# Attention and a gated feed-forward on one core: heads of a pair interleaved, transfers merged, and the planner's due times shifted

## The chip, the core and the metric

The kernel runs on one core of a Trainium2 chip. The metric is the device time of the whole program in microseconds. Before the change three runs took 1405.53, 1406.59 and 1406.96 us; the median is 1406.59 us.

## The reference

Attention over 8 batches, 12 heads, 448 positions and 64 channels, with q and k normalized by their root mean square, is followed by a two-layer network on 3584 tokens of 768 channels. The network's weights are drawn in double precision, q, k and v in single precision.

```python
q_n, k_n = rmsnorm(q, g_q), rmsnorm(k, g_k)
scores = q_n @ k_n.T / sqrt(64)
attn = exp(scores - max(scores))          # per row
attn = attn / (sum(attn) + 1e-9)
x = (attn @ v), heads put side by side    # 3584 x 768
h = x @ w_in                              # 3584 x 2048
out = (h * cos(h)) @ w_out                # 3584 x 768
```

## The kernel before

Heads are taken in 48 pairs, u = 0 to 47; a batch b is six pairs. Everything is held with channels on the partitions: one pair's q or k is a tile of 128 partitions (head 0's 64 channels, then head 1's) by 448 or 512 positions.

The first six pairs are "plain": their products are done in full single precision. All later pairs split each operand into a high part in the reduced format fp32r and the rest, a low part, and add two or three fast products. For a later pair, `prepare(u)` loads statistics input `sd`, k (`kd`) and q (`qd`), computes the norms (ACT squares, DVE reduces, GpSimd, named POOL, takes the power), sends the k norms to DRAM and back to spread them over partitions (`rkb`), scales k and q, and splits them: `khi`, `kl`, `qhi`, `ql`. Transfers then place them head by head: M holds a head's high k over its low k (64 partitions each), D the high q twice, E the low q. One matmul of M with D and one with E then give the complete score. M, D and E are rings of three heads.

`attend(u)` goes on: `score` (line 496 on) writes one of three PSUM banks S; `rowmin` (DVE, line 514) scales a tile of scores and takes its extreme; `expo` (ACT, line 522) writes the probabilities P and their sum. `transp` (lines 557 to 565) turns P in four chunks kc, each in two banks PT0 (four tiles) and PT1 (three). ACT casts a turned chunk to `hi` (`pt_high`, line 579), DVE subtracts to `lo` (`pt_low`, lines 586 and 588), and `av` (line 603) multiplies both with the split v into banks O0 and O1, one for each head. The ring of `hi` has two chunks, that of `lo` one. At the end of a pair `x_half` (ACT, line 637) copies half of an O bank into `xf` and `x_sum` (DVE, line 642) adds its other half; `x_norm` (POOL) applies the row sums. The next pair's first product needs the same two O banks.

`multiply(b)` computes h of a batch in 16 blocks fc of 18 matmuls each (`ffn1`, lines 672 to 674) in one PSUM bank `ph`; `h_out` (ACT, line 689) copies a block to one of two buffers `he`, and `h_store` writes it to DRAM, 224 KB each. `weights` decodes the double-precision w_in, 16 stages; `weights2` decodes quadrants of w_out, adds and splits them and stores seven combinations for the second plan.

No engine has its program written out. `add` gives each part of the work (a part is one function call) an engine, a cost, a due time, the keys it reads and writes, and for a transfer its KB. `Plan.order` then runs a list schedule: when an engine is free it takes, of the parts whose inputs are ready by the planner's own clock, the one with the earliest due time. The result is the fixed order on every engine; at run time each engine works its list in order and waits on semaphores. Transfers are all issued from SP. There are two plans, one up to the last attention pair (to about 930 us), and one for the rest of x times w_in and the second layer, which replaces eight products of half-size blocks by seven.

Of the kernel before, what the change touches and what calls it, by code (L numbers as in the profile page):

```python
# [23 lines left out]
class Plan:  # L24
# [11 lines left out]
    SLACK = 0.0  # L36
# [33 lines left out]
    def order(self):  # L70
# [27 lines left out]
        moved = 0.0  # L98
        self.busy = dict.fromkeys(free, 0.0)
        while True:  # L100
# [42 lines left out]
def tile_attention_moe(  # L143
# [4 lines left out]
    qT: bass.AP,  # L148
    kT: bass.AP,
# [8 lines left out]
    B, S, D = 8, kT.shape[2], 64  # L158
# [26 lines left out]
    h_d = dpool.tile([B, NFC, 128, S], F32, tag="h_d", name="h_d")  # L185
# [7 lines left out]
    gs = cpool.tile([128, 3], F32, tag="gs", name="gs")  # L193
    gsc = gs[:, 2:3]
# [5 lines left out]
    def g_load():  # L200
        nc.sync.dma_start(gs[:, 0:2], gg)

    def g_fold():
        nc.vector.scalar_tensor_tensor(
            gs[:, 2:3], gs[:, 0:1], -float(D) / math.sqrt(D), gs[:, 1:2], op0=ALU.mult, op1=ALU.mult
        )
# [4 lines left out]
        "sd": 1, "r": 5, "rkb": 1, "kd": 1, "kl": 1, "khi": 1, "qd": 1, "ql": 1, "qhi": 1, "M": 3, "D": 3, "E": 3, "vd": 1, "vs": 2, "S": 3, "sm": 3, "P": 11,  # L211
        "hi": 2, "lo": 1, "O0": 1, "O1": 1, "xf": 6, "rs": 1, "rt": 1, "ph": 1, "xsb": 1, "he": 2, "wf": 2, "rn": 1,
        "aq": 4, "at": 2, "ao": 1,
# [3 lines left out]
    RING.update(dict.fromkeys(PKEYS, 1))  # L217

    def w_load(fc):
        if f64:  # L220
            st = raw[fc] = wpool.tile([128, 2 * DM], I32, tag=f"w{fc}", name=f"raw{fc}")
            nc.sync.dma_start(st, w_in[fc].bitcast(I32))
        else:
            wfl[fc] = apool.tile([128, DM], F32, tag="wf", name=f"wf{fc}", bufs=RING["wf"])
            nc.sync.dma_start(wfl[fc], w_in[fc])
# [17 lines left out]
    def w_decode(fc, step):  # L243
        if step == 0:
            wfl[fc] = apool.tile([128, DM], F32, tag="wf", name=f"wf{fc}", bufs=RING["wf"])
        decode(raw[fc], wfl[fc], step)
# [12 lines left out]
    stage, quad, temp, part = {}, {}, {}, {}  # L259
# [12 lines left out]
    def v_quad(c, k):  # L272
        quad[(c, k)] = apool.tile([128, HM], F32, tag="aq", name=f"aq{c}_{k}", bufs=RING["aq"])
# [6 lines left out]
    def v_sum(c, j):  # L280
        if j < 2:
            temp[(c, j)] = apool.tile([128, HM], F32, tag="at", name=f"at{c}_{j}", bufs=RING["at"])
        a21, a22, a11, a12 = (quad.get((c, k)) for k in range(4))
        if j == 0:
            nc.vector.tensor_tensor(temp[(c, 0)], a21, a22, ALU.add)
        elif j == 1:
            nc.vector.tensor_tensor(temp[(c, 1)], temp[(c, 0)], a11, ALU.subtract)
        elif j == 2:
            nc.vector.tensor_tensor(a21, a11, a21, ALU.subtract)
        else:  # L290
            nc.vector.tensor_tensor(a11, a12, temp[(c, 1)], ALU.subtract)

    def v_split(c, p, src, lo):
        f = temp[(c, src - 4)] if src > 3 else quad[(c, src)]
# [14 lines left out]
    qlow = [apool.tile([128, 384], F32R, tag=f"E{i}", name=f"E{i}", bufs=1) for i in range(RING["E"])]  # L309
# [17 lines left out]
    def e_clear(i):  # L327
        nc.vector.tensor_scalar(
            qlow[i][64:128], ident[64:128, 0:1].broadcast_to([64, 384]), 0.0, 0.0, op0=ALU.mult, op1=ALU.add
# [49 lines left out]
    def kn_norm(u):  # L379
        x = pair[u]["kn"][:KB].rearrange("p (t d) -> p t d", d=D)  # L380
# [18 lines left out]

    def rk_load(u):  # L400
        spread(tl(u, "rkb", [128, S], F32), rk_d[u].rearrange("p t -> (p t)"))

    def k_load(u):
        nc.sync.dma_start(tl(u, "kd", [128, S], F32), kT[u])

    def k_norm(u):
        kd = pair[u]["kd"]
        kn = tl(u, "km", [128, S], F32, "M") if u < NP else kd
        nc.gpsimd.tensor_tensor(kn, kd, pair[u].pop("rkb"), ALU.mult)

    def k_high(u):
        khi, kd = tl(u, "khi", [128, 512], F32R), pair[u]["kd"]
        nc.scalar.copy(khi[:, 64:], kd)
        nc.scalar.copy(khi[64:, :64], kd[64:, 384:])

    def k_low(u):
        d = pair[u]
        kl, kd, khi = tl(u, "kl", [128, 512], F32R), d.pop("kd"), d["khi"].bitcast(F32)
        nc.gpsimd.tensor_tensor(kl[:, 64:], kd, khi[:, 64:], ALU.subtract)
        nc.gpsimd.tensor_tensor(kl[64:, :64], kd[64:, 384:], khi[64:, :64], ALU.subtract)  # L420
# [4 lines left out]
    def q_load(u):  # L425
        q = q_plain(u) if u < NP else tl(u, "qd", [128, 512], F32)
        nc.sync.dma_start(q, qT[u])

    def q_scale(u):
        q = q_plain(u) if u < NP else pair[u]["qd"]  # L430
        nc.gpsimd.tensor_scalar(q, q, gsc, 0.0, op0=ALU.mult, op1=ALU.add)

    def q_high(u):
        nc.scalar.copy(tl(u, "qhi", [128, 512], F32R), pair[u]["qd"])

    def q_low(u):
        d = pair[u]
        nc.gpsimd.tensor_tensor(tl(u, "ql", [128, 512], F32R), d.pop("qd"), d["qhi"].bitcast(F32), ALU.subtract)

    def m_place(u, h, low):  # L440
        if not low:
            pair[u]["M", h] = apool.tile([128, S], F32R, tag="M", name=f"M{u}_{h}", bufs=RING["M"])
        src = pair[u]["kl" if low else "khi"].bitcast(F32)[64 * h : 64 * h + 64, 64 - 64 * h : 512 - 64 * h]
        nc.sync.dma_start(pair[u]["M", h].bitcast(F32)[64 * low : 64 * low + 64], src)

    def d_place(u, h):
        t = pair[u]["D", h] = apool.tile([128, 384], F32R, tag="D", name=f"D{u}_{h}", bufs=RING["D"])
        src = pair[u]["qhi"].bitcast(F32)[64 * h : 64 * h + 64, :384]
        for a in (0, 64):
            nc.sync.dma_start(t.bitcast(F32)[a : a + 64], src)  # L450

    def e_place(u, h):
        t = pair[u]["E", h] = qlow[(2 * u + h) % RING["E"]]
        nc.sync.dma_start(t.bitcast(F32)[:64], pair[u]["ql"].bitcast(F32)[64 * h : 64 * h + 64, :384])

    def v_load(u, hh):
        nc.sync.dma_start(tl(u, f"vd{hh}", [128, NVC, D], F32, "vd"), v[u, :, hh * NVC : hh * NVC + NVC])
# [740 lines left out]
```

## Time and profile before

| | us |
|---|---|
| median of three runs | 1406.59 |
| the profiled execution | 1406.09 |
| its span, first to last instruction | 1404.3 |
| PE busy in the span | 1361.3 (97%) |
| DVE busy | 1085.0 (77%) |
| ACT busy | 937.2 (67%) |
| POOL busy | 671.0 (48%) |

An engine's busy time is drawn from its instructions; PE's matmuls are pipelined and their ends are modelled. A releaser is what ended an engine's idle time. Names of tiles are the program's, so O is a second product of attention, PT a turned chunk, ph a block of h.

### The profile page before, as it was taken

How to read it: one execution, taken by the hardware profiler on the slowest of the kernel's cores; microseconds unless marked ns; L12 is line 12 of the kernel's file. 1: busy time of each engine (PE TensorE's matmuls, PEld its weight loads, DVE VectorE, ACT ScalarE, POOL GpSimd, SP SyncE). 2: the span in 40 equal slices, each digit the busy share in tenths (PEclk: the TensorE clock that was granted, in tenths of full speed). 3: DMA queues.
4: the chain of work that ended last, by engine and by line, in shares of the span. 5: the costliest groups of instructions: out<-in, count | busy, mean ns of one | idle time of the engine just before them, and what ended most of it. 6: DMA issues, size and time to landing. Idle time of an engine off the chain costs nothing.

```text
span 1404.3 us, 22489 instructions
## 1 busy us (share of the span) xinstructions
PE 1361.3 (97%) x6992; PEld 1184.7 (84%) x6992; DVE 1085.0 (77%) x1864; ACT 937.2 (67%) x1910; POOL 671.0 (48%) x676
## 2 busy tenths in 40 slices
PE   6998999999999999999989999999999999999998
PEld 2445788888888898888979799999999999999998
DVE  7898989687787978778796976517879979879843
ACT  6677787777877877887777787637547457467331
POOL 5779886867866777786687676220000000000000
PEclk9999999999999999999999999999999999999999
DMA  5678767687877788777868776319788468468334
GB/s 201 210 230 241 193 174 221 195 251 222 239 218 236 209 242 229 231 231 217 247 195 253 210 215 196 85 52 352 274 295 291 166 219 296 156 228 288 132 110 149
DMA packets 169479, 301.89 MB, mean 215 GB/s; under 512 B 28512, under 2 KB 123568, under 8 KB 169360
## 3 DMA queue, kind: packets, MB, share of 16 engines
q1 hardware_dynamic: 169360, 300.45, 69.4%
q8 instruction: 56, 0.92, 0.3%
q14 instruction: 63, 0.52, 0.1%
HBM read 193.59 MB, written 62.73 MB: 183 GB/s over the span
## 4 chain that ended last, share of the span: by engine, by line
PE 69%; DVE 17%; ACT 5%; issue 4%; POOL 3%; DMA 2%; SPq 0%; DVEq 0%; ACTq 0%; POOLq 0%
PE y L743 10%; PE y L742 10%; PE y L744 10%; PE O L603 6%; PE ph L672 6%; PE ph L673 6%; PE ph L674 6%; PE S L510 5%; PE PT L557 5%; DVE S L514 4%; DVE lo L586 2%; ACT P L522 1%; DVE hi L588 1%; DVE aq L237 1%; DVE aq L235 1%
## 5 line engine op out<-in xcount | busy, mean ns | idle before, releaser
L522 ACT ACTIVATE P<-S,sm 128x448 f32<-128x448 f32 x336 | 212.7, 635 | 98.1 <-DVE S L514 92.9
L672 PE MATMUL ph<-xs,wi 128*128 128x448 f32 x660 | 252.3, 382 | 1.1 <-ACT he L689 1.1
L742 PE MATMUL y<-g,wo 128*128 128x448 f32 x672 | 245.4, 365 | 0.0
L744 PE MATMUL y<-g,wo 128*128 128x448 f32 x672 | 245.4, 365 | 0.0
L743 PE MATMUL y<-g,wo 128*128 128x448 f32 x672 | 245.4, 365 | 0.0
L514 DVE TENSOR_SCALAR_CACHE_REDUCE S<-S,r 128x448 f32<-128x448 f32 x336 | 223.7, 684 | 25.0 <-PE S L510 18.7
L673 PE MATMUL ph<-xs,wi 128*128 128x448 f32 x660 | 242.0, 367 | 0.0
L674 PE MATMUL ph<-xs,wi 128*128 128x448 f32 x660 | 241.6, 366 | 0.0
L724 ACT CAST g<-gq 128x896 fp32r<-128x896 f32 x112 | 105.6, 943 | 177.5 <-PE y L744 174.8
L586 DVE TENSOR_TENSOR lo<-PT,hi 128x512 fp32r<-128x512 f32 x252 | 149.0, 614 | 82.1 <-ACT hi L579 69.2
L579 ACT CAST hi<-PT 128x512 fp32r<-128x512 f32 (+1 forms) x336 | 170.2, 534 | 52.3 <-PE PT L563 27.8
L722 DVE TENSOR_TENSOR g<-gq,g 128x896 fp32r<-128x896 f32 x112 | 121.9, 1089 | 69.0 <-ACT g L724 68.4
L557 PEld LDWEIGHTS PT<-ident,P 128*128 128x128 f32 (+1 forms) x1050 | 125.8, 140 | 37.2 <-issue 22.9
L557 PE MATMUL PT<-ident,P 128*128 128x128 f32 (+1 forms) x1050 | 152.0, 276 | 0.0
L672 PEld LDWEIGHTS ph<-xs,wi 128*128 128x128 f32 x660 | 124.3, 188 | 13.2 <-ACT he L689 3.9
L743 PEld LDWEIGHTS y<-g,wo 128*128 128x128 f32 x672 | 126.2, 188 | 10.0
L744 PEld LDWEIGHTS y<-g,wo 128*128 128x128 f32 x672 | 126.2, 188 | 10.0
L742 PEld LDWEIGHTS y<-g,wo 128*128 128x128 f32 x672 | 126.2, 188 | 10.0
L674 PEld LDWEIGHTS ph<-xs,wi 128*128 128x128 f32 x660 | 124.3, 188 | 10.6
L673 PEld LDWEIGHTS ph<-xs,wi 128*128 128x128 f32 x660 | 124.6, 189 | 8.6
L359 POOL TENSOR_TENSOR r<-r,nhalf 128x14 f32<-128x14 f32 (+1 forms) x48 | 124.2, 2587 | 4.0
L603 PE MATMUL O<-hi,vs 128*128 128x448 f32 x336 | 120.3, 374 | 3.4 <-DVE hi L588 2.9
(116 smaller groups left out, 2705.6 us busy)
## 6 DMA issues: line engine op xcount, KB each, us to landing
wo<-wo_d SPq DMA_DIRECT2D x152, 384.0 KB
gq<-h_d SPq DMA_DIRECT2D x64, 448.0 KB
h_d<-he SPq DMA_DIRECT2D x120, 224.0 KB
wo_d<-ao SPq DMA_DIRECT2D x56, 384.0 KB
sd<-sd SPq DMA_DIRECT2D x46, 448.0 KB
D<-qhi SPq DMA_DIRECT2D x168, 96.0 KB
raw<-w_in SPq DMA_DIRECT2D x16, 768.0 KB
rawo<-w_out SPq DMA_DIRECT2D x32, 384.0 KB
```

What stands on the lines that cost most here:

```text
L514: nc.vector.tensor_scalar(d["S", t][:, :S], d["S", t][:, :S], d["r"][:, t : t + 1], None, op0=ALU.mult, op1=ALU.min, accum_out=d["sm"][:, ...
L522: nc.scalar.activation(p_rows(u, t), d.pop(("S", t))[:, :S], AF.Exp, bias=sm[:, 1, t : t + 1], scale=-1.0, accum_out=sm[:, 2, t : t + 1],)
L557: nc.tensor.transpose(pt[part][:n, i * 128 : i * 128 + 128], p_rows(u, t)[:, c : c + n], ident)
L579: nc.scalar.copy(hi if kc < 3 else hi[:64], pt_rows(u, kc, part))
L586: nc.vector.tensor_tensor(lo, src, hi.bitcast(F32), ALU.subtract)
L603: nc.tensor.matmul(O, st, d[what, kc][:, HEADS[hh]], start=(kc + n == 0), stop=(kc == 3))
L672: nc.tensor.matmul(ph[:, :S], whi, x2[:, 0, :], start=(cc == 0), stop=False)
L673: nc.tensor.matmul(ph[:, :S], whi, x2[:, 1, :], start=False, stop=False)
L674: nc.tensor.matmul(ph[:, :S], wlo, x2[:, 0, :], start=False, stop=(cc == NCC - 1))
L742: nc.tensor.matmul(y, whi, hi[:, e], start=first and e == 0, stop=False, **more)
L743: nc.tensor.matmul(y, whi, lo[:, e], start=False, stop=False, **more)
L744: nc.tensor.matmul(y, wlo, hi[:, e], start=False, stop=last and e == NG - 1, **more)
```

## The change

**Layout.** From pair 6 on the host puts the two heads' channels in turn, so partition 2d + h holds channel d of head h, and k and q stand side by side in one input, `kq`. One transfer loads both. One transfer spreads the k norms. M, D and E now hold both heads of a pair side by side in 64 (or twice 64) partitions, two pairs deep, so one transfer, or two for M, places what four or two did. v is loaded and split whole.

**Buffers.** The spread norms use room in M (later pairs) or D (plain pairs), `kq` is one buffer, the quadrants of w_out use three work buffers instead of four and two, and w_out's fetches one instead of two. The ring of `lo` has two chunks instead of one. The two `he` buffers are one tile, and two blocks of h are stored in one transfer, after the second.

**Planner.** It now counts eight transfers in flight at most, has a few new costs, and adds to each due time a number from a table by kind of part and by stage (0: pairs 9 and later, 1: the first three later pairs, 2: plain pairs; for blocks of h, batch 0 apart). The second plan has no such table.

The diff, cut to its core:

```diff
     FLY = 5.0
-    SLACK = 0.0
+    LANES = 8
+    TWICE = ("rk_spread", "rs_load", "d_place", "m_place")
...
+        landed = [0.0] * self.LANES
...
             if kb:
-                moved = max(moved, end) + kb / self.RATE
                 fly = self.FLIGHT.get(fn.__name__, self.FLY) if t > 12.0 else 2.4
-                done = max(end + fly, moved + 1.2)
+                half = 1 + (fn.__name__ in self.TWICE)
+                for i in range(half):
+                    end = max(end if i else t, landed.pop(0)) + cost / half
+                    moved = max(moved, end) + kb / half / self.RATE
+                    done = max(end + fly, moved + 1.2)
+                    landed.append(done + self.SIGNAL[e])
+                free[e] = max(end, landed[0])
...
-        "hi": 2, "lo": 1, "O0": 1, "O1": 1, "xf": 6, "rs": 1, "rt": 1, "ph": 1, "xsb": 1, "he": 2, "wf": 2, "rn": 1,
-        "aq": 4, "at": 2, "ao": 1,
+        "hi": 2, "lo": 2, "O0": 1, "O1": 1, "xf": 6, "rs": 1, "rt": 1, "ph": 1, "xsb": 1, "he": 2, "wf": 1, "wg": 1, "rn": 1,
+        "a0": 1, "a1": 1, "a2": 1, "ao": 1,
...
+    qtwo, qlow, kboth = keep("D", 768), keep("E", 768), keep("M", 2 * S)
+    kq = apool.tile([128, S + 512], F32, tag="kq", name="kq", bufs=1)
+    kd, qd = kq[:, :S], kq[:, S:]
...
+    def rk_load(u):
+        row = rk_d[u].rearrange("p t -> (p t)").rearrange("(o h s) -> o h s", o=1, h=2)
+        nc.sync.dma_start(rkb(u), row.broadcast_to([64, 2, S]))
...
+    def kq_load(u):
+        nc.sync.dma_start(kq, kq_in[u])
...
     def k_high(u):
-        khi, kd = tl(u, "khi", [128, 512], F32R), pair[u]["kd"]
-        nc.scalar.copy(khi[:, 64:], kd)
-        nc.scalar.copy(khi[64:, :64], kd[64:, 384:])
+        nc.scalar.copy(tl(u, "khi", [128, S], F32R), kd)
...
+    def m_place(u, low):
+        src = pair[u]["kl" if low else "khi"].bitcast(F32)
+        dst = kboth[u % 2].bitcast(F32)[64 * low : 64 * low + 64]
+        nc.sync.dma_start(dst[:, 384:512], src[:, 384:])
+        dst = bass.AP(dst.tensor, dst.offset, [dst.ap[0], [512, 2], [1, 384]])
+        nc.sync.dma_start(dst, src[:, :384])
...
+            nc.sync.dma_start(qtwo[u % 2].bitcast(F32)[a : a + 64], pair[u]["qhi"].bitcast(F32)[:, :384])
+    def e_place(u):
+        nc.sync.dma_start(qlow[u % 2].bitcast(F32)[:64], pair[u]["ql"].bitcast(F32)[:, :384])
...
+    hbuf = epool.tile([128, 2, S], F32, tag="he", name="hbuf", bufs=1)
...
+    def h_both(b, fc):
+        nc.sync.dma_start(h_d[b, fc // 2], hbuf)
...
-    add = plan.add
+    SHIFT = {
+        "av": (3.5, 10.0, 0.0), "av3": (7.0, 3.5, 0.0), "av_plain": (0.0, 0.0, 8.0), "d_place": (-8.0, 0.0, 0.0),
...
+    def add(eng, cost, due, fn, *args, **more):
...
+        plan.add(eng, cost, due + SHIFT.get(name, (0.0,) * 3)[stage], fn, *args, **more)
...
-            add(DVE, 0.61, due, rowmin, u, t, r=[("r", u)], w=[key, ("sm", u, 1, t)])
-            add(ACT, 0.62, due + 1, expo, u, t, r=[key, ("sm", u, 1, t)], w=[p_key(u, t), ("sm", u, 2, t)])
+            add(DVE, 0.65, due, rowmin, u, t, r=[("r", u)], w=[key, ("sm", u, 1, t)])
+            add(ACT, 0.65, due + 1, expo, u, t, r=[key, ("sm", u, 1, t)], w=[p_key(u, t), ("sm", u, 2, t)])
...
-                add(SP, ISS, d, h_store, b, fc, r=[home[fc]], kb=224.0)
+                if home[fc][0] != "he":
+                    add(SP, ISS, d, h_store, b, fc, r=[home[fc]], kb=224.0)
+                elif fc % 2:
+                    add(SP, ISS, d, h_both, b, fc, r=[("he", home[fc][1] - 1), home[fc]], kb=448.0)
```

**Where PE's order moves.** The place is the end of pair 23 and the first chunks of pair 24. In `O24_0` the first number is the pair, the second the head; in `hi24_0` the second is the chunk; S25 are scores of the next pair, `ph2_14` is block 14 of batch 2; a last number only counts buffers. Left out are rows of `ph` and of S. Before:

```order
L603 MATMUL O23_0_5187<-hi23_3_5336,vs23_4906 128x448
L603 MATMUL O23_1_5196<-hi23_3_5336,vs23_4906 128x448
...
L557 MATMUL PT0_103<-ident_88,P_102 128x128 x4
...
L557 MATMUL PT1_104<-ident_88,P_102 128x128 x3
L672 MATMUL ph2_14_5416<-xs_873,wi14_2037 128x448
...
L603 MATMUL O24_0_5450<-hi24_0_5414,vs24_5132 128x448
L603 MATMUL O24_0_5450<-lo24_0_5429,vs24_5132 128x448
L603 MATMUL O24_1_5454<-hi24_0_5414,vs24_5132 128x448
L603 MATMUL O24_1_5454<-lo24_0_5429,vs24_5132 128x448
L557 MATMUL PT0_103<-ident_88,P_102 128x128 x4
```

And now:

```order
L580 MATMUL PT0_110<-ident_88,P_107 128x128 x4
...
L580 MATMUL PT1_111<-ident_88,P_107 128x128 x3
L695 MATMUL ph2_14_4919<-xs_798,wi14_2061 128x448
...
L580 MATMUL PT0_110<-ident_88,P_107 128x128 x4
L626 MATMUL O23_0_4806<-hi23_3_4875,vs23_4595 128x448
L626 MATMUL O23_1_4810<-hi23_3_4875,vs23_4595 128x448
...
L588 MATMUL PT1_111<-ident_88,sm24_4665 7x128
...
L626 MATMUL O24_0_5015<-hi24_0_4926,vs24_4818 128x448
L626 MATMUL O24_0_5015<-lo24_0_4948,vs24_4818 128x448
```

Before, pair 23's last products stood ahead of pair 24's first turned chunk, and that chunk's products ahead of the next turn. Now the second chunk of pair 24 is turned first, pair 23's last products stand between, and pair 24's first product follows them after 11 matmuls and four transposes, where before 22 and seven stood between.

**Where SP's order moves.** SP issues all transfers. The place is the placement of pair 24's k and q. Left out are transfers of other kinds. Before:

```order
L444 DMA M24_0_4972<-khi24_4959 64x448
...
L450 DMA D24_0_4991<-qhi24_4974 64x384 x2
...
L444 DMA M24_0_4972<-kl24_4976 64x448
L454 DMA E0_99<-ql24_5001 64x384
...
L444 DMA M24_1_5108<-khi24_4959 64x448
L450 DMA D24_1_5111<-qhi24_4974 64x384 x2
L444 DMA M24_1_5108<-kl24_4976 64x448
L454 DMA E1_100<-ql24_5001 64x384
L692 DMA h_d_84<-he2_10_5120 128x448
```

And now:

```order
L719 DMA h_d_84<-hbuf_112 128x896
...
L476 DMA D0_100<-qhi24_4475 64x2x384 x2
L479 DMA E0_102<-ql24_4487 64x2x384
L470 DMA M0_104<-khi24_4521 64x2x64
L472 DMA M0_104<-khi24_4521 64x2x384
...
L470 DMA M0_104<-kl24_4548 64x2x64
L472 DMA M0_104<-kl24_4548 64x2x384
```

Ten transfers in two groups became seven in one, q ahead of k, and the store of h, here of two blocks, has 896 columns instead of 448.

## Rows read from the trace of the kernel before

**Rows 1.** Busy us and count per engine, PE clock, DMA share, GB/s, by stretch.

```profile
0.00:150.00 150.00, 130.04 (x538) 68.09 (x539) 126.91 (x252) 103.49 (x234) 117.52 (x107) 0.97 0.73 221
150.00:250.00 100.00, 92.42 (x495) 81.06 (x494) 91.16 (x174) 75.81 (x174) 77.73 (x76) 0.98 0.70 192
250.00:905.00 655.00, 643.10 (x3505) 576.62 (x3504) 505.58 (x1055) 500.38 (x1187) 466.66 (x487) 1.00 0.75 219
905.00:1400.70 495.70, 495.70 (x2460) 458.88 (x2458) 360.72 (x385) 257.53 (x316) 9.05 (x8) 1.00 0.62 213
1400.70:1404.30 3.60, 0.04 (x1) 0.00 (x0) 0.62 (x1) 0.00 (x0) 0.00 (x0) 0.77 0.35 127
```

**Rows 2.** PE groups by line: busy us, mean ns, idle us before, its releasers.

```profile
L603 PE MATMUL O<-hi,vs 128*128 128x448 f32 x336 | 120.3, 374 | 3.4 <-DVE hi L588 2.9 <-ACT hi L579 0.5
L510 PE MATMUL S<-M,D 128*128 128x448 f32 x252 | 99.0, 393 | 5.2 <-ACT P L522 5.0
L603 PE MATMUL O<-lo,vs 128*128 128x448 f32 x252 | 95.8, 380 | 11.0 <-DVE lo L586 10.5
...
L619 PE MATMUL O<-hi,vs 128*64 128x448 f32 (+1 forms) x96 | 45.0, 573 | 6.5 <-ACT hi L611 4.7 <-DVE hi L609 1.6
...
L510 PE MATMUL S<-khi,qhi 128*128 128x448 f32 x42 | 18.2, 433 | 2.6 <-ACT P L522 2.6
...
L387 PE MATMUL PT<-ident,kn 112*128 112x112 f32 x8 | 1.8, 371 | 7.7 <-DVE kn L382 7.7
```

**Rows 3.** Waits from 92 to 905 us: total us, times, longest.

```profile
PEld O L603 <- DVE lo L586: 21.1, 32, 2.2
...
PEld S L510 <- ACT P L522: 12.8, 16, 3.1
...
PEld O L603 <- DVE hi L588: 3.9, 4, 1.6
```

**Rows 4.** Timeline around 719 us: start us, us, instruction.

```profile
719.12 0.93 PE L557 MATMUL PT<-ident,P 128*128 128x128 f32 x7
```

**Rows 5.** ACT and DVE groups by shape: Casts and subtractions of turned chunks.

```profile
L579 ACT CAST hi<-PT 128x512 fp32r<-128x512 f32 x126 | 73.5, 584 | 21.1 <-PE PT L557 20.5
L579 ACT CAST hi<-PT 128x384 fp32r<-128x384 f32 x126 | 61.3, 486 | 2.7 <-PE PT L557 1.5 <-PE PT L565 0.9
...
L586 DVE TENSOR_TENSOR lo<-PT,hi 128x512 fp32r<-128x512 f32 x126 | 86.2, 684 | 79.3 <-ACT hi L579 66.6 <-PE O L603 12.0
L586 DVE TENSOR_TENSOR lo<-PT,hi 128x384 fp32r<-128x384 f32 x126 | 68.4, 543 | 2.7 <-ACT hi L579 2.6
```

**Rows 6.** Three stretches at the lower clock, columns as in rows 1.

```profile
33.90:40.70 6.80, 6.41 (x15) 2.43 (x15) 4.67 (x10) 3.68 (x6) 5.29 (x5) 0.50 0.54 154
85.10:88.50 3.40, 3.40 (x12) 1.86 (x11) 2.67 (x6) 2.58 (x6) 1.72 (x2) 0.50 0.87 296
160.20:163.60 3.40, 3.40 (x11) 3.00 (x11) 3.40 (x8) 2.94 (x8) 3.02 (x4) 0.50 0.69 184
```

**Rows 7.** ACT and DVE groups by shape: emptying the O banks.

```profile
L637 ACT COPY xf<-O 64x448 f32<-64x448 f32 x84 | 44.4, 528 | 7.7 <-PE O L603 5.5
L642 DVE TENSOR_TENSOR xf<-O,xf 64x448 f32<-64x448 f32 x84 | 52.1, 621 | 17.2 <-ACT xf L637 15.7
```

**Rows 8.** ACT's copies of h, and two transfers of the chain (start us, us).

```profile
L689 ACT ACTIVATE he<-ph 128x448 f32<-128x448 f32 x108 | 58.7, 543 | 26.2 <-PE ph L674 23.4 <-issue 2.2
...
135.31 6.17 DMA sd<-sd
...
477.21 2.31 DMA h_d<-he
```

**Rows 9.** Page: packets in all, and those of the queue that SP issues to.

```profile
DMA packets 169479, 301.89 MB, mean 215 GB/s; under 512 B 28512, under 2 KB 123568, under 8 KB 169360
...
q1 hardware_dynamic: 169360, 300.45, 69.4%
```

More of the change, by code (lines that the diff above doesn't have):

```diff
@@ L256, in w_low @@
         eng.tensor_tensor(w[:, 1, cs], wfl[fc][:, cs], w.bitcast(F32)[:, 0, cs], ALU.subtract)
-    stage, quad, temp, part = {}, {}, {}, {}
+    stage, quad, part = {}, {}, {}
     QUADS = ((0, 1), (1, 1), (0, 0), (1, 0))
@@ L308, in tile_attention_moe, with keep @@
     xs = {}
-    qlow = [apool.tile([128, 384], F32R, tag=f"E{i}", name=f"E{i}", bufs=1) for i in range(RING["E"])]
+    def keep(name, n):
+        return [apool.tile([128, n], F32R, tag=f"{name}{i}", name=f"{name}{i}", bufs=1) for i in range(2)]
+    qtwo, qlow, kboth = keep("D", 768), keep("E", 768), keep("M", 2 * S)
+    kq = apool.tile([128, S + 512], F32, tag="kq", name="kq", bufs=1)
+    kd, qd = kq[:, :S], kq[:, S:]
     pbuf = apool.tile([128, RING["P"], S], F32, tag="P", name="P", bufs=1)
@@ L359, in st_pow, with km, kn_rows @@
         nc.gpsimd.tensor_tensor(r, r, nhalf.broadcast_to([128, n]), ALU.pow)
+    kplain = [apool.tile([128, 2 * S], F32, tag="lo", name=f"km{i}", bufs=RING["lo"]) for i in range(2)]
+    def km(u):
+        return kplain[u % 2][:, HEADS[u % 4 // 2]]
     def kn_bank(u):
         return pt[u]
+    def kn_rows(u):
+        return (qd if u == 0 else pair[u]["kn"])[:KB]
     def kn_load(u):
-        nc.sync.dma_start(tl(u, "kn", [128, 512], F32, ("qd", "ql")[u])[:KB], kn_in[u])
+        if u:
+            tl(u, "kn", [128, 512], F32, "ql")
+        nc.sync.dma_start(kn_rows(u), kn_in[u])
     def kn_square(u):
-        nc.scalar.activation(kn_bank(u)[:KB], pair[u]["kn"][:KB], AF.Square)
+        nc.scalar.activation(kn_bank(u)[:KB], kn_rows(u), AF.Square)
     def kn_reduce(u):
@@ L436, in q_low @@
     def q_low(u):
[L437 to L444, printed above, removed]
@@ L798, in weights2 @@
         d = base(2 * NP) + c * span
-        qk = [("aq", 4 * c + k) for k in range(4)]
-        tk = [("at", 2 * c + j) for j in range(2)]
+        qk = [("a0", c), ("a1", c), ("a2", 2 * c), ("a2", 2 * c + 1)]
         for k in range(4):
-            st, f, e = ("wf", NFC + 4 * c + k), qk[k], d + 0.1 * span * k
+            st, f, e = ("wf", NFC // 2 + 4 * c + k), qk[k], d + span * (0.1 * k if k < 3 else 0.78)
+            over = [("wg", NFC // 2, k)] if c == 0 and k < 2 else []
             if f64:
@@ L806, in weights2 @@
                     add(eng, cost, e + step, v_decode, c, k, step,
-                        r=[st] if step != 3 else [], w=[f] if step != 3 else [st])
+                        r=[st] if step != 3 else [], w=[f, *over] if step != 3 else [st])
             else:
-                add(SP, ISS, e - 20.0, v_fetch, c, k, w=[f], kb=192.0, start=e - 30.0)
+                add(SP, ISS, e - 20.0, v_fetch, c, k, w=[f, *over], kb=192.0, start=e - 30.0)
         sums = (
-            (0, qk[0:2], [tk[0]]), (1, [tk[0], qk[2]], [tk[1]]),
-            (2, [qk[2]], [qk[0]]), (3, [qk[3], tk[1]], [qk[2]]),
+            (0, qk[0:1], qk[1:2]), (1, qk[2:3], qk[1:2]), (2, qk[2:3], qk[0:1]), (3, qk[1:2], qk[3:4]),
         )
-        made = {"P2": 0, "P4": 0, "P1": 0, "P5": 1, "P6": 2, "P7": 3, "P3": 4}
         done = 0
-        for n, (name, src, _) in enumerate(SPLITS):
-            e = d + span * (0.4 + 0.08 * n)
+        for n, (name, src, made, at) in enumerate(SPLITS):
+            e = d + span * (0.4 + 0.08 * at)
             p = PRODUCT[name]
-            while done < made[name]:
+            while done < made:
                 j, r, w = sums[done]
@@ L934, in attend @@
                 else:
-                    add(ACT, (0.49, 0.38)[half], dk + 1, pt_high, u, kc, half, **keys)
+                    add(ACT, (0.52, 0.43)[half], dk + 1, pt_high, u, kc, half, **keys)
                 if turn and half:
@@ L947, in attend @@
                     r = r + [("hi", m, 1)]
-                add(DVE, (0.6, 0.46)[half], dk + 2, pt_low, u, kc, half, r=r, w=w)
+                add(DVE, (0.64, 0.5)[half], dk + 2, pt_low, u, kc, half, r=r, w=w)
             for hh in range(2):
```

205 lines of the change are left out of this document (112 added, 93 removed), and 1 row of the table RING.

## The prediction

> **What bounds the kernel now.** I read the busy time by stage first [rows 1]. The reader is to see that TensorE (PE) is idle for 20.0 us of the first 150 us, 7.6 us of the next 100, 11.9 us of the 655 us that end the first plan, 0.0 us of the 496 us of the second plan, and 3.6 us at the end: 43.0 us of a 1404.3 us span. The change leaves the second plan's arithmetic alone and removes no matmul, so all that it can win or lose is idle time of PE in the first plan, at most about 39 us.
>
> Next, PE's groups by line [rows 2], to see what the idle time stands in front of. 7.7 us is the very first transpose, which waits for the norm of k. The second products (tile O) of the later pairs wait 11.0 us in front of the low parts and 3.4 us in front of the high parts of the turned probabilities, the first six pairs' second products 6.5 us, and the scores 7.8 us (5.2 and 2.6) for the Exp that empties a score bank.
>
> Third, the waits of the weight load in the stretch of the later pairs [rows 3]: 21.1 us in 32 waits and 3.9 us in 4 for O, 12.8 us in 16 for scores. These are larger than PE's own, because a matmul's end is modelled: in the second plan 2460 matmuls take 495.7 us, one every 0.20 us [rows 1], while each is drawn 0.37 to 0.39 us long [rows 2], so the first 0.17 us or so of a stall are drawn as busy. A weight load runs one matmul ahead and can be late by about 0.2 us for nothing. So the O waits really cost (21.1 + 3.9) - 36 x 0.2 = 17.8 us, between the 14.4 us of rows 2 and the 25.0 us of rows 3, and the scores' 12.8 - 16 x 0.2 = 9.6 us. I use these.
>
> **The O waits (main term).** Between a transpose and the product that uses it stand two Casts on ScalarE (ACT), 0.58 and 0.49 us, and two subtractions on VectorE (DVE), 0.68 and 0.54 us [rows 5], each chain behind whatever its engine has just begun: some 2.3 us, where first parts overlap second ones less. In PE's order of before, pair 24's first chunk has 12 matmuls of x times w_in between its second group of transposes and the first product of O24: 12 x 0.2 = 2.4 us. That is no reserve. In the changed order the transposes of the next chunk go first, and from the first chunk's second group to O24's first product stand 26 matmuls, 5.2 us, and eight transposes, of which seven take 0.93 us [rows 4]: about 6.2 us. Of all chunks the third keeps the least, by the order about 4 us. A late Cast or subtraction then hides behind PE's work. I take three quarters of 17.8 us: -13.5 us, with ends -17.8 us and 0.
>
> **The score waits.** They stand in the first 250 us, where DVE is busy 87% (126.9 + 91.2 of 250) [rows 1]. Scores keep their three banks and stand about as far apart as before, but what DVE and ACT do ahead of them is reordered. -2.5 us, ends -9.6 us and +4 us.
>
> **The first six pairs.** The opening rows of all five engines are the same kinds of work in the same order, so the 7.7 us stays. The products come later behind their transposes, which takes from the 6.5 us, but the next chunk's transposes now come closer behind the last one's and need their bank emptied by one Cast of 0.58 us [rows 5]. -1 us, ends -6.5 and +4 us.
>
> **The clock.** In three stretches of 6.8, 3.4 and 3.4 us the granted clock is 0.50, the 1.2 GHz level, otherwise 2.4 GHz [rows 6]; each follows idle time of PE. At half clock at most half of each stretch is lost, 6.8 us in all. With fewer stalls one of the short ones may go: -1.5 us, ends -6.8 us and +3.4 us.
>
> **What the change pays: the O banks.** Because products move back, the last product of pair 23 now stands 11 matmuls and four transposes before the first of pair 24 in the same bank, 2.2 + 0.5 = 2.7 us, where before it was 22 and seven, 4.4 + 0.9 = 5.3 us. In between ACT must copy half the bank (0.53 us) and DVE add the other half (0.62 us) [rows 7], with signals and with work already begun on each about 2 to 2.5 us. By the order about 15 of the 41 changes of pair are this tight. An O wait of before cost 17.8 / 36 = 0.5 us on average; if nine of the 15 wait, 9 x 0.5 = +4.5 us, ends 0 and 15 x 2.2 us (the longest wait in rows 3) = +33 us.
>
> **The paired store.** Two h blocks now leave in one transfer of 448 KB, out of the only buffer, so the next h_out (0.54 us, rows 8) waits until it has landed. A stretch of 224 KB of h on the chain took 2.31 us, one of 448 KB of statistics input 6.17 us [rows 8]. From the end of one block's matmuls to the end of the next block's stand by the order some 36 matmuls, 7.2 us. The h_out of 0.54 us, issue and signals of an estimated 0.8 us and a landing of 2.31 us make 3.6 us, which costs nothing; a landing of 6.17 us makes 7.5 us, 0.3 us late, of which the matmuls that follow before the bank is wanted take most. There are 54 such stores. +1 us, ends 0 and 54 x 0.5 = +27 us.
>
> **Edits that cost nothing on the path.** One load for k and q, one for v, one broadcast load, whole-pair placements: the queue issues fewer transfers, and no PE wait of rows 2 is ended by a transfer. POOL loses the small k_low subtraction and two of four v instructions per pair, ACT the small k_high copy; POOL and ACT are idle over a fifth of each later stretch [rows 1], so the gain is hidden under PE. w_out's stages now pass through one fetch buffer and three work buffers; their results are needed only in the second plan, so the cover is the rest of the first plan. If it failed, the wait would stand where the second plan places its first weights, in a stretch where PE now waits for nothing. The second buffer of lo is part of the main term.
>
> The two-part placement of k writes rows of 64 columns, 256 bytes: 84 placements by 128 rows are 10,752 more packets under 512 bytes, beside 28,512 before [rows 9]. The queue's packets took 69.4% of 16 engines, 0.69 x 16 x 1404 / 169,360 = 0.092 us each on average; merged rows of k, q, v and h save at least as many packets. The Trainium skill, "DMA: Bandwidth & Descriptors", section "Specifications", says that a transfer under 512 bytes falls short of line rate because the engine reads, modifies and writes. No row here prices a short packet alone. By the average of the rows the sum is the one below; if by that rule each short packet cost twice the average, the placements would add 10,752 x 0.184 / 16 = 124 us of queue time over some 800 us, an estimate that lifts the queue's share of 0.75 to 0.90 and leaves the sum, but makes rival B below likelier: without it I would give B 0.10.
>
> **Sum.** -13.5 - 2.5 - 1 - 1.5 + 4.5 + 1 = -13 us. The profiled execution took 1406.09 us, 1.8 us more than its span; 1406.1 - 13 = 1393.1, and the median of the runs is 0.5 us above the profiled one. Forecast 1393 us.
>
> **Rivals.** (A) The wait only moves: all 15 tight bank changes cost 1 us each, 15 us instead of 4.5; 1406.6 - 13 + 10.5 = 1404 us, within what can be told from no change. For it: the two-step emptying of O and 11 matmuls of room; against it: both steps are short [rows 7]. (B) Slower: the 448 KB store becomes the clock of the x times w_in blocks. If it lands after 7 us or more as a rule, h_out is late by 0.6 us or more, ACT holds the Exps behind it, and PE waits for the one block bank 54 times. It decides from 13 / 54 = 0.24 us of wait per store; at 0.4 us each it gives 1393 + 54 x 0.4 = 1415 us. For it: the 6.17 us stretch, a queue busy 0.75 of the time [rows 1]; against it: the 2.31 us stretch, and fewer transfers ahead of it. (C) More is won: all 17.8 us, 6 us of the scores, 1 us of the first pairs, 4 us of clock, with 3 us for banks and stores: 1406.6 - 25.8 = 1381 us. For it: nothing that waits on PE's path then is left but the start. Against it: DVE at 87% early.
>
> **Chances.** Forecast (its own range 1385 to 1402) 0.65, C 0.12, A 0.10, B 0.13. A measurement of this kernel can tell about 0.2% (2.8 us) from no change. Faster 0.77, same 0.10, slower 0.13. The range from 1382 to 1409 leaves out part of C and most of B.
>
> **What would show it.** Right: PE idle before O's low parts under 4 us and the weight load's wait under 7 us in the later pairs; PE idle from 250 to 905 us under 6 us; a new idle time in front of O's high parts released by the second half's addition into xf, about 4 us; no PE wait released by a transfer. Wrong: waits of ph released by the h_out Cast of more than 5 us in sum, with ACT waiting for the store (B); O waits released by xf of more than 12 us (A); a later first transpose, or more half-clock stretches than three.

## The result and the profile after

Four runs of the changed kernel took 1384.37 to 1387.4 us, median 1385.34 us; four of the kernel before, 1405.53 to 1410.73 us, median 1406.78 us. The ratio is 0.9845, 95% interval 0.9822 to 0.9867: 21.4 us faster. That lies in the range, but the gain was forecast as 13 us, and most of it came from another place than the one forecast. That the total came near is in good part luck.

The profiled execution took 1385.76 us with a span of 1383.7 us, 20.6 us less than before: PE's idle time fell from 43.0 to 31.0 us, its drawn busy time from 1361.3 to 1352.7 us.

First the stretches of the first plan in the changed kernel; columns as in [rows 1].

```profile
0.00:150.00 150.00, 136.14 (x579) 72.78 (x580) 130.03 (x260) 106.64 (x241) 117.71 (x99) 1.00 0.82 232
150.00:250.00 100.00, 97.36 (x539) 87.32 (x538) 92.18 (x173) 81.98 (x185) 84.66 (x70) 1.00 0.77 191
250.00:905.00 655.00, 644.56 (x3539) 580.69 (x3538) 515.45 (x1065) 485.93 (x1151) 429.64 (x378) 1.00 0.82 218
```

PE is idle 13.9 us in the first 150 (20.0 before), 2.6 in the next 100 (7.6) and 10.4 in the long stretch (11.9). In the first 250 us PE now does 1118 matmuls instead of 1033. The granted clock is 1.00 in each row: the three stretches at 0.50 of [rows 6] are gone.

Second, PE's groups by line in the changed kernel, the counterpart of [rows 2].

```profile
L695 PE MATMUL ph<-xs,wi 128*128 128x448 f32 x660 | 251.8, 382 | 3.5 <-ACT hbuf L713 3.5
...
L580 PE MATMUL PT<-ident,P 128*128 128x128 f32 (+1 forms) x1050 | 163.9, 275 | 8.6 <-DVE lo L609 4.2 <-DVE rt L558 2.1 <-DVE hi L632 0.8
L626 PE MATMUL O<-hi,vs 128*128 128x448 f32 x336 | 122.9, 381 | 0.7 <-DVE xf L665 0.7
L533 PE MATMUL S<-M,D 128*128 128x448 f32 x252 | 101.7, 404 | 0.4 <-ACT P L545 0.4
...
L626 PE MATMUL O<-lo,vs 128*128 128x448 f32 x252 | 92.1, 365 | 1.0 <-DVE lo L609 1.0
L642 PE MATMUL O<-hi,vs 128*64 128x448 f32 (+1 forms) x96 | 43.7, 557 | 0.0
...
L585 PE MATMUL PT<-ident,P 128*128 128x128 f32 x126 | 21.1, 276 | 2.9 <-DVE lo L609 2.8
L533 PE MATMUL S<-khi,qhi 128*128 128x448 f32 x42 | 16.0, 381 | 0.0
...
L413 PE MATMUL PT<-ident,kq 112*128 112x112 f32 x4 | 1.0, 400 | 7.7 <-DVE kq L408 7.7
```

The O waits of later pairs fell from 14.4 to 1.7 us, scores from 7.8 to 0.4, the first six pairs' O from 6.5 to 0. The transposes, which had no row with idle time of their own, now wait 8.6 and 2.9 us, 7.0 us of it for the subtraction that writes `lo` and so frees the turned chunk's bank. Third, the weight load's and PE's waits from 92 to 905 us (total us, times, longest), as in [rows 3]:

```profile
PEld PT L580 <- DVE lo L609: 9.0, 14, 1.6
...
PEld ph L695 <- ACT hbuf L713: 6.2, 9, 1.7
...
PEld PT L585 <- DVE lo L609: 5.8, 9, 1.7
...
PEld O L626 <- DVE lo L609: 1.7, 2, 1.0
PEld O L626 <- DVE xf L665: 1.1, 1, 1.1
```

The 32 waits of O for `lo` became two, and 23 waits for the same subtraction stand in front of the transposes.

The second plan's first product (y<-g,wo) starts at 992.00 us before and at 970.64 us after, so the gain is all in the first plan. To place it, I counted PE's work in each trace, 0.203 us for a matmul of 448 columns, 0.109 us for a transpose, 0.45 and 0.43 us for the first six pairs' scores and products, and read when 250 us of it were done. That is at about 300 us; "early" below is the change of this time against before, "rest" the change from there to the second plan's first product. Each is one execution, and runs of one kernel spread by 1 to 14 us; read at 280 to 300 us instead, after's early part is 15.4 to 16.4 us and e14's 5.4 to 7.2, and the others move by at most 1 us. The traced executions of e6, e2, e4 and e14 are 2.0 to 4.5 us slower than their kernels' medians, that of e3 is 2.8 us faster. The last four columns are the weight load's waits for another engine in the same trace, in us, from 250 us to the second plan's first product, by what PE does next: `O`, `PT` or `ph`, and the sum of all (with the scores).

| kernel | median, us | early | rest | O | PT | ph | all |
|---|---|---|---|---|---|---|---|
| before | 1406.78 | 0 | 0 | 20.6 | 0.2 | 3.9 | 27.6 |
| after | 1385.34 | -14.2 | -7.2 | 1.5 | 14.6 | 4.2 | 22.3 |
| table left out (e1) | 1391.81 | -8.6 | -7.9 | 12.4 | 0.2 | 3.9 | 19.5 |
| table for later pairs alone (e2) | 1387.28 | -11.5 | -5.8 | 2.9 | 8.5 | 5.9 | 20.1 |
| table for early pairs alone (e3) | 1400.82 | -14.4 | +3.7 | 14.7 | 0.5 | 12.5 | 31.4 |
| table left out, one lo (e11) | 1392.5 | -9.9 | -6.3 | 11.5 | 0.2 | 5.9 | 20.5 |
| one lo (e6) | 1400.34 | -6.9 | +4.9 | 0.8 | 19.2 | 8.4 | 33.1 |
| before with table (e4) | 1403.39 | -5.9 | +5.1 | 1.1 | 23.1 | 6.4 | 35.8 |
| before with two lo (e12) | 1402.61 | -1.3 | -2.4 | 15.9 | 1.2 | 4.3 | 25.8 |
| before with two lo and table (e14) | 1410.24 | -6.1 | +12.5 | 8.6 | 16.4 | 9.4 | 44.6 |

The change of the last column against before follows "rest" to about 2 us, but for e4 (8.2 beside 5.1) and e14 (17.0 beside 12.5).

### The profile page after: what moved, and what is told of

Read it like the earlier page. It is cut to its first block, busy times and chain, and to the rows that moved or that the text cites. A ratio compares the mean times of both kernels' runs of the same rounds, so it can differ in the third digit from the quotient of the medians.

```text
span 1383.7 us, 21527 instructions
## 1 busy us (share of the span) xinstructions
PE 1352.7 (98%) x6992; PEld 1179.9 (85%) x6992; DVE 1089.8 (79%) x1863; ACT 921.2 (67%) x1868; POOL 637.7 (46%) x550
## 2 busy tenths in 40 slices
DMA packets 149472, 301.80 MB, mean 218 GB/s; under 512 B 34368, under 2 KB 83088, under 8 KB 149360
## 3 DMA queue, kind: packets, MB, share of 16 engines
q1 hardware_dynamic: 149360, 300.43, 74.8%
## 5 line engine op out<-in xcount | busy, mean ns | idle before, releaser
L602 ACT CAST hi<-PT 128x512 fp32r<-128x512 f32 (+3 forms) x336 | 175.1, 531 | 60.3 <-PE PT L580 33.9
L580 PE MATMUL PT<-ident,P 128*128 128x128 f32 (+1 forms) x1050 | 163.9, 275 | 8.6 <-DVE lo L609 4.2
L609 DVE TENSOR_TENSOR lo<-PT,hi 128x512 fp32r<-128x512 f32 x252 | 151.9, 618 | 17.0 <-ACT hi L602 15.1
L770 PEld LDWEIGHTS y<-g,wo 128*128 128x128 f32 x672 | 126.2, 188 | 10.9 <-DVE g L749 0.9
```

What stands on the lines that cost most here:

```text
L580: nc.tensor.transpose(pt[part][:n, i * 128 : i * 128 + 128], p_rows(u, t)[:, c : c + n], ident)
L602: nc.scalar.copy(hi if kc < 3 else hi[:64], pt_rows(u, kc, part))
L609: nc.vector.tensor_tensor(lo, src, hi.bitcast(F32), ALU.subtract)
L770: nc.tensor.matmul(y, whi, lo[:, e], start=False, stop=False, **more)
```

## The experiments

Three theories: the order (the table takes the O waits away), the buffer (the second `lo`), and the layout (fewer and larger transfers, less work on POOL and ACT). In these texts "the layout" also brings the planner's new costs, which no run takes out of the new layout, and its limit, which e9 takes out. Times before were 1407.47 us beside the first four, 1407.0 beside the next four (e5, e6, e9, e10) and 1407.82 beside the last four (e11 to e14). Ratios are to these, with 95% intervals.

**e1_no_shift.** The table is not added:

```diff
-        plan.add(eng, cost, due + SHIFT.get(name, (0.0,) * 3)[stage], fn, *args, **more)
+        plan.add(eng, cost, due, fn, *args, **more)
```

> The changed kernel with the table of shifted due times left out (all shifts 0); layout, buffers, merged transfers and the planner's new costs stay. Order theory (the shifted due times win the time, by putting products behind the next turn): 1400 us, 1396 to 1405, with over 8 us of PE idle in front of O's low and high parts of the later pairs. Layout theory (merged transfers, the second buffer of lo and the lighter POOL win it): 1388 us, 1384 to 1392, with O waits as small as after the change (1.7 us).

Measured 1391.81 us (1391.48 to 1392.09), 0.9887 [0.9872, 0.9902]. PE's group, as before:

```profile
L626 PE MATMUL O<-lo,vs 128*128 128x448 f32 x252 | 94.7, 376 | 7.5 <-DVE lo L609 7.5
```

The O waits are mostly back (7.5 us for the low parts, 2.0 for the high ones), yet 15.7 of the 21.4 us stay. The table is worth some 6 us. The order theory's sign came (over 8 us in front of O), but not its time, so it falls as the main cause; the layout theory had the time, but not the sign.

**e2_later_only** and **e3_early_only.** The shifts of stage 0 alone (pairs 9 and later), and those of stages 1 and 2 alone:

```diff
-        plan.add(eng, cost, due + SHIFT.get(name, (0.0,) * 3)[stage], fn, *args, **more)
+        plan.add(eng, cost, due + SHIFT.get(name, (0.0,) * 3)[stage] * (stage == 0), fn, *args, **more)
```

In e3 the factor is `(stage > 0)`.

> The table's shifts only for stage 0 (pairs 9 and later, blocks of h from batch 1, weights); the first nine pairs are unshifted. Order theory: 1391 us, 1387 to 1396: the O waits stay away after 250 us, but PE loses about 4 us more before 200 us and one or two stretches at the 1.2 GHz level come back. Layout theory: 1386 us, within 2 us of the changed kernel. If the early part is worth more than the clock and 4 us, over 1396 us.

> The table's shifts only for stages 1 and 2 (first nine pairs); stage 0 unshifted. Order theory: 1396 us, 1391 to 1401, with PE idle of 10 us or more between 250 and 905 us in front of O. Layout theory: 1386 us, PE idle there as after the change (10.4 us) and in front of the transposes.

Measured: e2 1387.28 us (1382.82 to 1389.62), 0.9851 [0.9831, 0.9871]; e3 1400.82 us (1398.03 to 1406.2), 0.9955 [0.9942, 0.9968]. e2 can't be told from after. e3 gets its early 14.4 us like after, and then loses 3.7 us in the rest, with 8.5 us of waits in front of O's low parts. The two halves don't add up (e1 is faster than e3): a list schedule is a new order for every table, so one part of the table has no price of its own. What e3 loses in the rest stands in front of ph, 12.5 us of the weight load's waits where e1 has 3.9.

**e4_old_layout_shift.** The kernel before, with the table as it stands (kinds of part that it doesn't have get no shift):

```diff
-    add = plan.add
+    SHIFT = { ... }
+    def add(eng, cost, due, fn, *args, **more):
...
+        plan.add(eng, cost, due + SHIFT.get(name, (0.0,) * 3)[stage], fn, *args, **more)
```

> The kernel before, in its layout with its transfers, buffers and planner, with the table of shifted due times added. Order theory: 1393 us, 1389 to 1399 (the one buffer of lo limits how far products can stand behind the turn, so some of the 21 us is missing). Layout theory: 1404 us, 1400 to 1408.

Measured 1403.39 us (1400.13 to 1407.94), 0.9968 [0.9956, 0.998]. PE's groups:

```profile
L557 PE MATMUL PT<-ident,P 128*128 128x128 f32 (+1 forms) x1050 | 156.8, 277 | 18.6 <-DVE lo L586 12.2 <-DVE hi L588 3.0 <-ACT hi L611 1.0
...
L603 PE MATMUL O<-lo,vs 128*128 128x448 f32 x252 | 92.6, 367 | 0.4 <-DVE lo L586 0.4
...
L562 PE MATMUL PT<-ident,P 128*128 128x128 f32 x126 | 21.0, 275 | 4.3 <-DVE lo L586 4.3
```

The table does what the prediction read from the order: 0.4 us is left of the 11.0 us in front of O's low parts [rows 2]. But 22.9 us now stand in front of the transposes, where before nothing did, 16.5 us of it for `lo`. The subtraction that was late for O is as late for the bank that the next chunk is turned into.

**e6_lo_one.** After, with one `lo` in the plan and in memory; the plain k that shared the second buffer gets one of its own:

```diff
-        "hi": 2, "lo": 2, ...
+        "hi": 2, "lo": 1, ...
-    kplain = [apool.tile([128, 2 * S], F32, tag="lo", name=f"km{i}", bufs=RING["lo"]) for i in range(2)]
+    kplain = [apool.tile([128, 2 * S], F32, tag=("lo", "km1")[i], name=f"km{i}", bufs=1) for i in range(2)]
```

> The changed kernel with one buffer for lo again, in the planner's rings and in memory (the plain pairs' k moves to a buffer of its own); table, layout and transfers stay. Buffer theory (with one lo, products that stand behind the next turn hold lo, lo holds the PT banks, and the waits move to the transposes): 1396 us, 1391 to 1402, with 17 us or more of PE idle in front of transposes. Layout theory without the buffer: 1386 us, 1383 to 1389, transposes as after the change (11.5 us).

Measured 1400.34 us (1398.55 to 1404.89), 0.9956 [0.9942, 0.9971]: 15 us of the gain are gone. PE's group:

```profile
L580 PE MATMUL PT<-ident,P 128*128 128x128 f32 (+1 forms) x1050 | 160.1, 277 | 11.0 <-DVE lo L609 9.1 <-DVE hi L632 0.8 <-DVE rt L558 0.4
```

The time is the buffer theory's; its sign is missed: 15.0 us in front of transposes (11.0 and 4.0 in the two groups) where 17 or more was said, and 11.5 in after.

**e11_lo_one_no_shift.** e6 with e1's edit: neither second `lo` nor table.

> The changed kernel with one buffer for lo and with no table. Buffer theory (the second lo is what the change lives on, and merged transfers by themselves win little): 1404 us, 1400 to 1408, near the kernel before. Layout theory (merged transfers and the lighter POOL win most of the 15 us that the layout without the table showed): 1394 us, 1391 to 1398.

Measured 1392.5 us (1390.83 to 1394.81), 0.9893 [0.9873, 0.9914], not told apart from e1. So in the new layout the second `lo` alone wins nothing, and the table with one `lo` loses 8 us; only both together win, some 7 us. Layout and planner without both win 15 us. Its stretches:

```profile
0.00:150.00 150.00, 131.53 (x567) 70.93 (x568) 127.14 (x258) 105.27 (x240) 110.67 (x98) 1.00 0.83 229
150.00:250.00 100.00, 96.97 (x525) 85.51 (x524) 94.37 (x172) 81.20 (x184) 83.23 (x68) 1.00 0.80 192
```

By 250 us 1092 matmuls are done, 59 more than before, with neither of the two edits on which the main term rested.

**e12_old_two_lo** and **e14_old_two_lo_shift.** The kernel before with a second `lo`, paid for by after's w_out buffers (one fetch, three work buffers, and their order of splits); e14 adds e4's edit.

```diff
-        "hi": 2, "lo": 1, "O0": 1, "O1": 1, "xf": 6, "rs": 1, "rt": 1, "ph": 1, "xsb": 1, "he": 2, "wf": 2, "rn": 1,
-        "aq": 4, "at": 2, "ao": 1,
+        "hi": 2, "lo": 2, "O0": 1, "O1": 1, "xf": 6, "rs": 1, "rt": 1, "ph": 1, "xsb": 1, "he": 2, "wf": 1, "wg": 1, "rn": 1,
+        "a0": 1, "a1": 1, "a2": 1, "ao": 1,
```

> The kernel before with two buffers for lo and nothing else of the change but what pays for their room (w_out's quadrants in three work buffers, one fetch buffer); old transfers, old planner, no table. Buffer theory: 1393 us, 1389 to 1398, as the new layout without the table (1391.8 us). Layout theory: 1404 us, 1401 to 1408.

> The kernel before with two buffers for lo as in the run beside it, and with the table of shifted due times; old transfers and old planner. Buffer theory: 1388 us, 1384 to 1393, with PE idle in front of transposes under 12 us (it was 22.9 us with the table and one lo). Layout theory: 1399 us, 1395 to 1404.

Measured: e12 1402.61 us (1401.05 to 1405.81), 0.9966 [0.9954, 0.9978]; e14 1410.24 us (1403.46 to 1417.35), 1.0017 [0.9997, 1.0037]. On the old layout the pair of edits wins nothing; e12's 5 us may come from the w_out part as well. Its early stretch stays as before (1.3 us), while the table on the old layout gains 5.9 and 6.1 us early (e4, e14). e14 came out slower than both theories had it. Its transposes wait 12.9 us instead of e4's 22.9, near the buffer theory's 12, but PE now idles 9.2 us in front of ph and 4.1 us for xf, where e4 has 2.6 and 0.7.

**e9_no_lanes.** After, with the planner's limit of eight transfers in flight lifted.

```diff
-    LANES = 8
+    LANES = 4096
```

> The changed kernel with the planner's bound of eight transfers in flight taken out of its reckoning (set to 4096); the program's own limit at run time stays. Planner theory (the order fits because transfers are planned as they can run): 1394 us, 1389 to 1400. Layout theory: 1386 us, 1383 to 1390, since with so few transfers the bound seldom bites.

Measured 1385.88 us (1383.38 to 1391.53), 0.9861 [0.9832, 0.9889]: no difference from after. The limit wins nothing here.

**e10_old_new_planner.** The kernel before, its planner given the limit and the new costs, no table:

```diff
+    LANES = 8
...
-                moved = max(moved, end) + kb / self.RATE
...
+                    end = max(end if i else t, landed.pop(0)) + cost / half
...
-            add(DVE, 0.61, due, rowmin, u, t, r=[("r", u)], w=[key, ("sm", u, 1, t)])
+            add(DVE, 0.65, due, rowmin, u, t, r=[("r", u)], w=[key, ("sm", u, 1, t)])
```

> The kernel before with the changed planner alone: eight transfers in flight and the new costs of rowmin, expo, pt_high, pt_low and x_norm; layout, transfers and buffers of before, no table. Planner theory: 1396 us, 1391 to 1401, since the unshifted order of the new layout took 1391.8 us. Layout theory: 1406 us, 1402 to 1410.

Measured 1505.41 us (1504.25 to 1510.68), 1.0709 [1.0688, 1.0731]: 98 us slower, which no theory had. Its long stretch, and one PE group:

```profile
250.00:905.00 655.00, 590.07 (x2992) 507.93 (x2993) 456.90 (x936) 438.67 (x1023) 406.20 (x426) 0.96 0.67 196
```

```profile
L610 PE MATMUL O<-hi,vs 128*128 128x448 f32 x336 | 132.4, 403 | 24.3 <-DVE hi L595 19.3 <-ACT hi L586 2.3 <-DMA vd<-v 1.5
```

The instructions are those of before; only their order differs. The DMA share is 0.67, below before's 0.75 [rows 1], so a full queue isn't the bound: PE waits for DVE and ACT. In the new layout, with seven placements for ten and fewer loads, the same limit does no harm (e9). That the planner holds the limit to be binding with the old transfers and not with the new, and so orders the lists for a late queue, is an inference from the two times; the limit and the new costs stand in one run here, and which of them does the harm is not shown.

**e5_single_store.** After, with each block of h stored by itself:

```diff
-                if home[fc][0] != "he":
-                    add(SP, ISS, d, h_store, b, fc, r=[home[fc]], kb=224.0)
-                elif fc % 2:
-                    add(SP, ISS, d, h_both, b, fc, r=[("he", home[fc][1] - 1), home[fc]], kb=448.0)
+                add(SP, ISS, d, h_store, b, fc, r=[home[fc]], kb=224.0)
```

> The changed kernel with every block of h stored by itself (224 KB, each block's half of the buffer free when its own store has landed). If the paired store costs what PE idles in front of ph (3.5 us, the h_out Cast as releaser): 1382 us, 1379 to 1385. If it costs nothing that matters, as the forecast had it (+1 us): 1385 us, 1382 to 1388. If fewer transfers are what the change lives on: 1389 us or more, for 54 transfers come back.

Measured 1382.67 us (1381.53 to 1389.29), 0.9839 [0.9814, 0.9864]. The wait in front of ph falls from 3.5 to 1.8 us; the time can't be told from after's.

**e13_single_no_lanes.** e5 and e9 together, as a version that might beat both.

> The changed kernel with single stores of h and without the planner's bound of eight transfers in flight: the two edits that did not hurt by themselves. 1382 us, 1379 to 1385; if the two orders only differ by chance, anything from 1381 to 1388.

Measured 1380.05 us (1377.59 to 1383.88), 0.9799 [0.978, 0.9819]: all five runs lie below the lowest of after (1384.37), 27.8 us below before. Since neither edit is clear alone, this may be a luckier order rather than two causes.

## Why the prediction was right or wrong

**O waits (-13.5 us): the effect came, the gain did not.** The step said that a late Cast or subtraction then hides behind PE's work. For O it does (14.4 to 1.7 us of PE's own waits). What it left out is that the same subtraction empties the bank of the turned chunk, and that the next transposes, moved ahead, want that bank: 11.5 us of new waits in after, 22.9 us in e4. This is rival A, a wait that only moves, but to the transposes, not to the O banks where I looked. The table of kernels shows it each time the shifts of the later pairs are added: from e1 to after the weight load's waits for O fall by 10.9 us and those for PT rise by 14.4; from e1 to e2 by 9.5 and 8.3, from before to e4 by 19.5 and 22.9, from e11 to e6 by 10.7 and 19.0, from e12 to e14 by 7.3 and 15.2. The rest of the first plan then changes by +0.7, +2.1, +5.1, +11.2 and +14.9 us. From e3 to after it falls by 10.9 us, but there too O's 13.2 us go to PT (14.1); what falls is ph, by 8.3 us. So the step's exchange won nothing where the term was placed. What the table won, 5.6 us from e1 to after, it won early. The second `lo`, priced as part of this term, does what it can only in combination: with two, in the new layout, the table is harmless in the later pairs.

Part of the term's waits did go, by another cause. Without the table, e1 and e11 have 12.4 and 11.5 us for O instead of 20.6, and nothing new in front of PT; their rest is 7.9 and 6.3 us shorter. So layout and planner take 8 to 9 us of the O waits without a wait in their place; which part of them does it is not shown.

**Edits that cost nothing (0): the other step that failed.** I priced lighter POOL and ACT work and fewer transfers at nothing because POOL is idle over a fifth of each later stretch. Together with the planner's limit and costs they won 15 us without table and second `lo` (e11), 9.9 of it early. The reason given holds from 150 us on, but not from 92 to 150 us. The first row is before's, the second e11's, with the columns of [rows 1]:

```profile
92.00:150.00 58.00, 51.49 (x253) 35.69 (x250) 51.66 (x99) 44.21 (x100) 54.92 (x51) 1.00 0.79 230
92.00:150.00 58.00, 52.29 (x262) 37.83 (x262) 49.24 (x97) 44.26 (x103) 49.65 (x44) 1.00 0.96 238
```

POOL is busy 54.92 of 58 us there, and the timeline of before shows once how that reaches PE (start, us; in brackets the idle time before and its releaser):

```profile
111.36 1.63 POOL L645 TENSOR_TENSOR xf<-xf,rs 128x448 f32<-128x448 f32 x1
...
113.02 0.56 ACT L654 CAST xs<-xf 128x448 fp32r<-128x448 f32 x1 [2.29 <-POOL xf L645]
113.49 0.58 ACT L611 COPY hi<-PT 128x512 f32<-128x512 f32 x1
...
114.12 0.97 PE L619 MATMUL O<-hi,vs 128*64 128x448 f32 x2 [2.66 <-ACT hi L611]
```

ACT takes its list in order, so while it waits 2.29 us for POOL's xf, the copy that PE needs stands behind it, and PE idles 2.66 us. PE's row names ACT, not POOL; only ACT's row of xs does. But this is not where e11's early gain lies: PE idles 6.5 us of this stretch before and 5.7 us in e11. In after POOL is as busy (54.34 us), and PE idles 2.8 us.

Read by the same count of PE's work, e11 gains 5.5 us on the work that before does from 29 to 45 us, 1.3 us on what follows up to 156 us, and 3.9 us on that from 156 to 170 us; after gains 5.8, 3.4 and 4.0 us. In the first and the last of these PE of before stalls, and then runs at the lower clock of [rows 6], 33.9 to 40.7 us and 160.2 to 163.6 us:

```profile
33.28 1.15 PE L619 MATMUL O<-hi,vs 64*64 64x448 f32 x2 [1.86 <-ACT hi L611]
...
159.60 0.47 PE L510 MATMUL S<-M,D 128*128 128x448 f32 x1 [2.21 <-ACT P L522]
```

In the second of them products of x times w_in start 0.37 us apart, after it 0.20 us. e11 has neither stall, and runs the same stretches at full clock:

```profile
33.90:40.70 6.80, 6.80 (x31) 2.65 (x29) 6.74 (x14) 5.66 (x11) 3.51 (x4) 1.00 0.58 155
160.20:163.60 3.40, 3.40 (x19) 2.91 (x18) 3.33 (x6) 2.68 (x5) 2.24 (x3) 1.00 1.05 245
```

So do e4 (first row) and e10 (second), both with the old layout, in the first stretch:

```profile
33.90:40.70 6.80, 5.99 (x31) 2.83 (x29) 6.74 (x9) 5.05 (x11) 5.04 (x5) 1.00 0.41 123
33.90:40.70 6.80, 6.80 (x31) 2.89 (x30) 6.66 (x14) 6.57 (x12) 4.04 (x3) 1.00 0.71 200
```

On the work from 29 to 45 us e4 gains 4.6 us and e10 4.1 us; e12, which still runs there at a clock of 0.54, gains 0.1 us. So this first part of the early gain comes to the old layout too, with another order alone, without merged transfers or lighter POOL; what gives the rest of it is not shown. POOL's splits of v and k over the 42 later pairs did fall from 106.2 and 68.5 us to 85.4 and 55.3 us, 34 us in all, but no run sets a price on them alone.

**Scores (-2.5 us) and first six pairs (-1 us): right in kind, too small.** The scores' drawn waits fell by 7.4 us, the first pairs' by 6.5. Both are early stalls, and e1 shows the layout takes part of each (scores 4.2 us left, first pairs 2.7), the table the rest. **Clock (-1.5 us):** all three stretches went, up to 6.8 us, in after as in e11; they followed stalls of the same early stage, so stall and clock are one gain counted in two terms. These three reached the far ends of their ranges, together about -20 us, which is the size of the whole gain; but drawn waits don't add up to the time.

**O banks (+4.5 us): 0.7 us,** one wait, so a room of 2.7 us was mostly enough for the copy and the addition. **Paired store (+1 us):** 2.4 us more wait in front of ph, ACT waiting for h's store 1.8 us in two waits; rival B did not come. (The weight load's waits for h_out are 6.2 us, over the 5 us named, but in nine waits, and ACT waited for a store only in those two.) **No PE wait released by a transfer** holds, and the first transpose waits 7.7 us as before.

**The signs.** O's low parts under 4 us (1.0) and the weight load's wait under 7 us (1.7) came out as said. PE idle under 6 us from 250 to 905 us did not (10.4), nor the 4 us released by xf (0.7). The result lies at the edge of the forecast's own range, between it and rival C (1381 us), with C's content in scores, first pairs and clock. Two errors of opposite sign, a main term whose exchange won nothing and 15 us from edits priced at nothing, brought the sum near it.

**Open:** which part of layout and planner gives the rest of the early time and takes the 8 to 9 us of O waits, and how much of any single order is chance.

## What to carry to other kernels

When an engine's wait is taken away, follow the ring that the late instruction also empties: its next user inherits the wait. Here a second buffer paid only together with the order that uses it, and only in the new layout. Before edits are priced at nothing, read the stage by a window no wider than it, and then check where the time really came: a busy engine beside a waiting one is not yet the cause. A stall of about 2 us that is followed by some us at the lower clock costs more than itself; an order that merely avoids it can win what looks like the gain of a layout. A planner's new costs and limits belong to the transfers that they were made with: moved to the old program, they cost more than any other edit here.

## What the runs showed of the hardware

The changed kernel moves the same bytes in fewer packets, but they take longer:

```profile
DMA packets 149472, 301.80 MB, mean 218 GB/s; under 512 B 34368, under 2 KB 83088, under 8 KB 149360
...
q1 hardware_dynamic: 149360, 300.43, 74.8%
```

Beside [rows 9], the queue's packets fell by 20,010 and their share of 16 engines rose from 69.4% to 74.8%: 0.748 x 16 x 1383.7 / 149,360 = 0.111 us each instead of 0.092, in sum 60 us more per engine. The packets' own times in the two traces show where it comes from. The two-part placement of k added 10,752 packets of 256 bytes, as the prediction counted, but each took 0.027 us on average, 18 us per engine in all; the prediction's 124 us, at twice the average for each, did not come. (Packets under 512 bytes rose by only 5,856, because 4,896 packets of 4 bytes went.) The Trainium skill, "DMA: Bandwidth & Descriptors", section "Specifications", says that a transfer under 512 bytes falls short of line rate, and the trace agrees: 256 bytes in 0.027 us are 9 bytes per ns, where packets of 3,072 bytes move 21 (0.144 us). More of the queue's time is in the other rows of the placements, of 1,536 bytes: 16,128 packets of 0.101 us became 26,880 of 0.130 us, 102 and 219 us per engine, partly in place of rows of 1,792 bytes. Why a row of the same size took longer is not shown. No PE wait came of it: the stretch from 250 to 905 us ran at a DMA share of 0.82 (0.75 before) without a transfer releasing PE.
